# Short last tiles of a mixture of experts by plain float32 matmuls on column groups, and an overflow count taken in mid-kernel

## The chip, the cores and the metric

The kernel runs on one core of a Trainium2 chip. The metric is the device time of one execution in microseconds (us). The engines are named as the profile names them: PE (TensorE, matmuls; PEld its weight loads), DVE (VectorE), ACT (ScalarE), POOL (GpSimd) and SP (SyncE, which here issues the DMAs). PSUM is the memory that matmuls write; it has eight banks of 512 float32 numbers in each of 128 partitions.

## What is computed

Attention within chunks of 64 tokens, and behind it a mixture of experts in which a gate with noise sends each of 4608 tokens to two of eight experts:

```python
def _moe_ref(x, w_gate, w_noise, noise, w1, w2) -> np.ndarray:
    logits = x @ w_gate
    noise_scale = np.log1p(np.exp(x @ w_noise))
    noisy_logits = logits + noise_scale * noise
    top2 = np.argpartition(-noisy_logits, 2, axis=1)[:, :2]
    ...
    for e in range(E):
        for k in range(2):
            mask = top2[:, k] == e
            ...
            h = np.maximum(x[mask] @ w1[e], 0.0)
            out[mask] += top2_w[mask, k, None] * (h @ w2[e])
```

Here x is 4608 x 512, W1 of an expert 512 x 1024 and W2 1024 x 512, all float32.

## The kernel before

The first quarter of the kernel is the attention (`attend`, L593), in token tiles of 128, together with the gate and the scattering of token rows to lists in DRAM, one list for each expert. From about 166 us on the expert layers run. The experts are taken in slots 0 to 7, sorted by how many tokens they have, and each slot has a fixed capacity (`CAPS`, L30): 1216 rows for slots 0 and 1, 1184 for 2 to 4, 1152 for 5 to 7. What does not fit is done by a loop at the end that runs only if the count of overflowing tiles is above zero (L773; it is zero here).

A capacity is cut into tiles of 128 rows, and the tiles into three blocks for each expert (`blocks_of`, L39). 1216 rows leave a last tile of 64 rows, 1184 one of 32, and 1152 none. Such a last tile is the fourth tile of its expert's third block.

Every matrix product is made of three matmuls. A float32 number is split into a high part and a rest, both of type float32r: `hi` is a copy made by ACT, `lo` the difference made by DVE (`w_split`, L113, for weights; L276 and L277 for hidden values). `three` (L256) then multiplies hi by hi, hi by lo and lo by hi. In layer 1 (`layer1`, L265) a piece of W1 is the stationary operand, and the rows of the whole block, 384 to 448, stream past it: 96 matmuls a block. In layer 2 (`layer2`, L286) a tile of hidden values, 128 deep and r rows wide, is stationary, and W2 streams past it in 512 columns, which makes 24 matmuls a tile whatever r is. `weigh` (L280) scales the tile by the gate's weights on DVE, and POOL adds it to the output by an indirect DMA (`store`, L228).

The order of the work is written out by hand; each engine runs its instructions in program order. The main loop (L678) has an iteration for each block i, and in it layer 1 of block i and then layer 2 of block i - 1. Work for later is hung between the matmuls by hooks:

- the next block's x tiles are transposed and split (`x_tile`, L237), in layer 1 or, in the iteration of an expert's second block, in layer 2 of its first one; each such turn lets SP gather one more tile, seven tiles ahead (`gather_more`, L220);
- raw W2 of an expert is split during layer 1 of its second block (L697), and raw W1 of the next expert during layer 2 of its second block, which runs in the iteration of the third (L704).

Raw weights lie in four buffers of the pool `stage` (L97), 512 KB each, used in turn: four pieces of W2 of expert e, then four of W1 of e + 1, then four of W2 of e + 1. `w_load` (L103) issues a load on SP, and it waits there until the buffer's last reader is done. W1 of the next expert is issued at the head of the iteration of the second block (L682), W2 of the next expert at the end of the iteration of the third (L751).

A count read into a register (`values_load`, L772, which the profile calls TENSOR_LOAD) is done by every engine for itself. It stands at the very end, behind nine small DVE steps that compute the count (L759 to L770).

Of the kernel before, what the change touches and what calls it, by code (L numbers as in the profile page):

```python
# [8 lines left out]
FT = mybir.dt.float32  # L9
FR = mybir.dt.float32r  # L10
BF = mybir.dt.bfloat16
I32 = mybir.dt.int32
U32 = mybir.dt.uint32
AF = mybir.ActivationFunctionType
OP = mybir.AluOpType
AX = mybir.AxisListType
# [3 lines left out]
P = 128  # L20
NTOK = 4608
NT = NTOK // P
DM = 512
NE = 8
FF = 1024
ND = DM // P
NF = FF // P
# [8 lines left out]
CLEAN = max(CAPS) - P  # L36


def blocks_of(cap):  # L39

    rows = [min(P, cap - s) for s in range(0, cap, P)]
    out, cur = [], []
    for j, r in enumerate(rows):
        cur.append((j, r))
        if len(cur) == 3 and len(rows) - j - 1 != 1:
            out.append(cur)
            cur = []
    if cur:
        out.append(cur)
    return out  # L50


# [1 line left out]
def kernel(ctx, tc, qT, kT, vh, wgn, noise, w1, w2, out, caps=CAPS):  # L54
    nc = tc.nc
    consts = ctx.enter_context(tc.tile_pool(name="consts", bufs=1))
# [16 lines left out]
    e_row = consts.tile([P, NE], FT, name="e_row")  # L73
# [10 lines left out]
    cape = consts.tile([P, NE], FT, name="cape")  # L84
# [3 lines left out]
    for c in sorted(set(caps[1:])):  # L88
        n = caps.index(c, 1)
        nc.vector.memset(caprow[:, n:n + caps[1:].count(c)], float(c))  # L90
    nc.vector.memset(caprow[:, 0:1], float(caps[0]))
    run8 = consts.tile([P, NE], FT, name="run8")
# [5 lines left out]
    W = {}  # L98
    staged = {}
# [3 lines left out]
    def w_load(e, which, c):  # L103
        st = stage.tile([P, 1024], FT, name="st")
        staged[e, which, c] = st
        if which == 1:
            nc.sync.dma_start(st, w1v[ds(place[e], 1), c].rearrange("o j r f -> (o j) r f") if e else w1[e, c * P:(c + 1) * P, :])  # L107
        else:
            nc.sync.dma_start(st.rearrange("p (f n) -> p f n", f=2),
                              w2[ds(place[e], 1) if e else slice(0, 1), 2 * c * P:(2 * c + 2) * P, :]  # L110
                              .rearrange("o (f p) n -> p (o f) n", f=2))
# [14 lines left out]

    blocks = [blocks_of(c) for c in caps]
    nb = len(blocks[0])  # L130
    assert all(len(b) == nb for b in blocks)
    BL = [(e, b) for e in range(NE) for b in range(nb)]
    NBL = len(BL)
# [6 lines left out]
    NPE = nb  # L140
# [14 lines left out]
    XG, XH, HT, BX, BH, OB = {}, {}, {}, {}, {}, {}  # L155
# [14 lines left out]
    def weights_of(i, j):  # L170
        e = BL[i][0]
        k = j - blocks[0][i][0][0] if i in EARLY else 0
        return lwt0[i][:, k:k + 1] if i in EARLY else lwt[:, j, e:e + 1]
# [37 lines left out]
    def gather(i):  # L211
        for k in range(len(blocks[BL[i][0]][BL[i][1]])):
            gather_tile(i, k)
# [42 lines left out]
    def three(p, w, w_s, x, x_s, first, last, flip=False):  # L256

        (wh, wl), (xh, xl) = w, x
        for n, (a, b) in enumerate(((wh, xh), (wh, xl), (wl, xh)) if not flip else ((wh, xh), (wl, xh), (wh, xl))):
            a, b = a[w_s], b[x_s]  # L260
            if flip:
                a, b = b, a
            nc.tensor.matmul(p, a, b, start=first and n == 0, stop=last and n == 2)  # L263

    def layer1(i, hook, hook_d=lambda f, d: None):  # L265
        e, b = BL[i]
        n = sum(r for _, r in blocks[e][b])
        HT[i] = BH[0 if i == 1 else i % 2]
        for f in range(NF):
            p = bank("l1", (0, 1) if i == 0 else None)[:, 0:n]  # L270
            for d in range(ND):
                three(p, W[e, 1, d], (slice(None), slice(f * P, (f + 1) * P)),
                      XH[i], (slice(None), d, slice(0, n)), d == 0, d == ND - 1)
                hook_d(f, d)
            hh, hl = HT[i][f]
            nc.scalar.activation(hh[:, 0:n], p, AF.Relu)  # L276
            nc.vector.scalar_tensor_tensor(hl[:, 0:n], p, 0.0, hh[:, 0:n].bitcast(FT), op0=OP.max, op1=OP.subtract)  # L277
            hook(f)

    def weigh(i, j, r, p):  # L280
        e = BL[i][0]
        o = OB[0].tile([P, DM], FT, name="o")
        nc.vector.tensor_scalar(o[0:r], p[0:r], weights_of(i, j)[0:r], None, op0=OP.mult)  # L283
        store(i, e, j, r, o)

    def layer2(i, hook):  # L286
        e, b = BL[i]
        tiles = blocks[e][b]
        for k, (j, r) in enumerate(tiles):
            p = bank("l2")  # L290
            for f in range(NF):
                three(p[0:r], W[e, 2, f // 2], (slice(None), slice((f % 2) * DM, (f % 2) * DM + DM)),
                      HT[i][f], (slice(None), slice(k * P, k * P + r)), f == 0, f == NF - 1, flip=True)
                hook(k, f)
            weigh(i, j, r, p)


    pa = ExitStack()
    pk = ExitStack()
# [377 lines left out]

    for i in range(NBL + 1):  # L678
        e, b = BL[i] if i < NBL else (NE, 0)
        if i == 2:  # L680
            gather_more(2)
        if b == 1 % nb and e + 1 < NE and i > 1:  # L682
            for c in range(4):
                w_load(e + 1, 1, c)
        split2 = halves if i < NBL and (b == 1 % nb if e else b == 0) else []
        nxt = blocks[BL[i + 1][0]][BL[i + 1][1]] if i + 1 < NBL else []

        def turn_next(k):
            x_tile(i + 1, k)
            ahead[0] -= 1  # L690
            gather_more(2)

        def hook1(f):
            if i > 1 and b != 1 and f % 2 == 1 and f // 2 < len(nxt):
                turn_next(f // 2)
            if split2:
                w_split(e, 2, *split2[f])  # L697
            if i == 0:
                scatter(2, HT[0][f][0][0:1, 0:1].bitcast(FT))

        def hook2_f(k, f):
            if i > 1 and b == 1 and f % 4 == 1 and 2 * k + f // 4 < len(nxt):
                turn_next(2 * k + f // 4)
            if (k, f) == (0, 3):  # L704
                for q in split1:
                    w_split(split1_e, 1, *q)

        def hook2_r(k, f):
            hook2_f(k, f)
            step_route(2)  # L710
            if f % 2 == 0:
                scatter(1)
            if (k, f) in TURNS[i]:
                x_tile(i + 1, TURNS[i].index((k, f)))

        if 1 < i < NBL and i == 3:
            resolve_all()
            layer2(i - 1, hook2_f)
        if i < NBL:
            layer1(i, hook1, hook_tail if i == 0 else lambda f, d: None)  # L720
        split1 = halves if (i < NBL and b == nb - 1 and e + 1 < NE) else []
        split1_e = e + 1

        if i == 0:
            pa.close()
            block_x(1)
            OB[0] = pb.enter_context(tc.tile_pool(name="ob", bufs=4))
        if i == 0:
            zero_out(NT)
            resolve_early(0)  # L730
            layer2(0, hook2_r)
            finish_route()
            last_rows.close()
            block_h(1)
            for r in range(1, NE):
                place[r] = nc.values_load(order[0:1, r:r + 1], engines=[mybir.EngineType.SP], min_val=0, max_val=NE - 1)
            for c in range(4):
                w_load(1, 1, c)
            pg.close()
            later_xg.append(pb.enter_context(tc.tile_pool(name="xg2", bufs=3)))  # L740
            xy = pb.enter_context(tc.tile_pool(name="xy", bufs=2))
            gather(3)
            for r in range(NE):
                nc.sync.dma_start(meta[:, :, r], by_slot[0:NJ * P, ds(place[r], 1) if r else slice(0, 1), CODE:USED]
                                  .rearrange("(j p) o c -> p j (o c)", p=P))
        elif i == 1:
            resolve_early(1)
            layer2(1, hook2_r)
        elif i != 2 and i != 3:
            layer2(i - 1, hook2_f)  # L750
        if split1:  # L751
            for c in range(4):
                w_load(e + 1, 2, c)
# [1 line left out]


    ovp = ctx.enter_context(tc.tile_pool(name="ovp", bufs=1))
    nf = ovp.tile([P, NE], FT, name="nf")
    nc.vector.tensor_sub(nf, run8, e_row)  # L759
    nc.vector.tensor_scalar(nf, nf, 1.0 / NE, float(P - 1), op0=OP.mult, op1=OP.add)  # L760
    nc.vector.tensor_sub(nf, nf, cape)
    nt = ovp.tile([P, NE], I32, name="nt")
    nc.vector.tensor_copy(nt, nf)
    nc.vector.tensor_scalar(nt, nt, 7, None, op0=OP.arith_shift_right)
    nc.vector.tensor_copy(nf, nt)
    nc.vector.tensor_scalar(nf, nf, 0.0, None, op0=OP.max)
    tot = ovp.tile([1, 1], FT, name="tot")
    nc.vector.tensor_reduce(tot, nf[0:1], AX.X, OP.add)
    toti = ovp.tile([1, 1], I32, name="toti")
    nc.vector.tensor_copy(toti, tot)  # L770
    MT = 80
    n_over = nc.values_load(toti[0:1, 0:1], min_val=0, max_val=MT)  # L772
    with tc.If(n_over > 0):  # L773
        it_row = ovp.tile([P, MT], FT, name="it_row")
        nc.gpsimd.iota(it_row, pattern=[[1, MT]], base=0, channel_multiplier=0, allow_small_or_imprecise_dtypes=True)
# [112 lines left out]
```

## Time and profile before

| | us |
|---|---|
| median of 3 runs | 1030.37 (1027.99 to 1031.94) |
| the profiled execution | 1029.36 |
| its span | 1027.6 |
| PE busy in the span | 983.1 (96%) |
| DVE, ACT, POOL busy | 446.1 (43%), 271.3 (26%), 227.4 (22%) |
| DMA from HBM and to it | 81.69 MB read, 50.13 MB written |

The span runs from the first to the last instruction that the profile saw. Ends of matmuls are modelled and overlap, so the time between the starts of two matmuls tells what one costs, and their "mean ns" does not. A float32 matmul (not float32r) shows as two records.

### The profile page before, as it was taken

The page shows a single profiled execution, that of the slowest core. Times are in us where ns is not written, and L with a number is a line of the kernel's source. Part 1 is how long each engine was busy: PE and PEld are TensorE (multiplying, and loading weights), DVE is VectorE, ACT ScalarE, POOL GpSimd, SP SyncE. Part 2 cuts the span into 40 slices and gives each one's busy share as a digit, 9 for nine tenths or more (in the row PEclk, how much of TensorE's full clock was granted, in tenths as well). Part 3 has the DMA queues.
Part 4 walks back from the last instruction along what each step waited for, and adds up shares of the span by engine and source line. Part 5 has one row for each costly group of instructions (what it writes and reads, how often), then busy time and mean ns, then how long its engine had stood idle before and what let it go on. Part 6 is the DMA issues. An engine that isn't in the chain of part 4 may idle for free.

```text
span 1027.6 us, 16132 instructions
## 1 busy us (share of the span) xinstructions
PE 983.1 (96%) x5962; PEld 883.5 (86%) x5962; DVE 446.1 (43%) x1005; ACT 271.3 (26%) x542; POOL 227.4 (22%) x332
## 2 busy tenths in 40 slices
PE   6889998999799999999999999999999999999996
PEld 6778887898689889888988998899889998999884
DVE  6656665522525443344334432453245324533311
ACT  3434443211314121222222321232123212322100
POOL 3034754751020111111111102101211111101112
PEclk9999999999899999999999999999999999999998
DMA  8899999864561552264225422553244324412213
GB/s 226 259 292 298 328 323 396 310 177 121 88 166 56 124 117 37 60 140 116 40 46 138 124 40 44 125 135 59 36 121 123 74 43 126 120 21 32 31 21 43
DMA packets 103218, 132.93 MB, mean 129 GB/s; under 512 B 22848, under 2 KB 56000, under 8 KB 103136
## 3 DMA queue, kind: packets, MB, share of 16 engines
q1 hardware_dynamic: 86704, 93.54, 30.4%
q0 software_dynamic: 16432, 38.33, 19.1%
q8 instruction: 48, 0.79, 0.3%
q14 instruction: 34, 0.28, 0.1%
HBM read 81.69 MB, written 50.13 MB: 128 GB/s over the span
## 4 chain that ended last, share of the span: by engine, by line
PE 84%; SPq 6%; DMA 5%; DVE 2%; issue 2%; ACT 1%; POOL 0%; DVEq 0%; ACTq 0%; POOLq 0%
PE PS L263 78%; DMA kb<-in_kT 2%; PE PS L381 2%; SPq L322 1%; PE PS L355 1%; SPq L327 1%; DMA xg<-slots 1%; DMA vb<-in_vh 1%; SPq L207 1%; PE PS L409 1%; PE PS L371 1%; SPq L320 1%; DMA out<-zero 1%; PE PS L396 1%; SPq L107 0%
## 5 line engine op out<-in xcount | busy, mean ns | idle before, releaser
L263 PE MATMUL PS<-xh,w1h 128*128 128x384 f32 (+2 forms) x768 | 262.6, 342 | 9.4 <-DVE hl L277 6.2
L230 POOL DMA_INDIRECT out<-o,lid x77 | 119.3, 1549 | 684.5 <-DVE o L283 680.3
L263 PE MATMUL PS<-xh,w1l 128*128 128x384 f32 (+2 forms) x768 | 261.7, 341 | 0.0
L263 PE MATMUL PS<-xl,w1h 128*128 128x384 f32 (+2 forms) x768 | 261.6, 341 | 0.0
L263 PE MATMUL PS<-w2h,hh 128*128 128x512 f32 x616 | 240.5, 390 | 0.0
L263 PE MATMUL PS<-w2h,hl 128*128 128x512 f32 x616 | 240.2, 390 | 0.0
L263 PE MATMUL PS<-w2l,hh 128*128 128x512 f32 x616 | 240.2, 390 | 0.0
L276 ACT ACTIVATE hh<-PS 128x384 fp32r<-128x384 f32 (+2 forms) x192 | 95.0, 496 | 481.0 <-PE PS L263 425.4
L277 DVE SCALAR_TENSOR_TENSOR hl<-PS,hh 128x384 fp32r<-128x384 f32 (+2 forms) x192 | 108.5, 566 | 188.4 <-ACT hh L276 185.5
L283 DVE TENSOR_SCALAR o<-PS,lwt 128x512 f32<-128x512 f32 x77 | 57.7, 749 | 248.6 <-PE PS L263 246.2
L263 PEld LDWEIGHTS PS<-xh,w1h 128*128 128x128 f32 x768 | 145.3, 189 | 12.7 <-DVE hl L277 6.6
L263 PEld LDWEIGHTS PS<-xl,w1h 128*128 128x128 f32 x768 | 145.4, 189 | 1.9
L263 PEld LDWEIGHTS PS<-xh,w1l 128*128 128x128 f32 x768 | 145.2, 189 | 1.1
L263 PEld LDWEIGHTS PS<-w2h,hl 128*128 128x128 f32 x616 | 112.9, 183 | 27.2
L263 PEld LDWEIGHTS PS<-w2l,hh 128*128 128x128 f32 x616 | 112.9, 183 | 26.2
L263 PEld LDWEIGHTS PS<-w2h,hh 128*128 128x128 f32 x616 | 112.9, 183 | 25.8
L532 POOL DMA_INDIRECT slots<-xs,lii x72 | 72.5, 1007 | 26.5 <-issue 20.8
L253 ACT ACTIVATE xh<-y 128x512 fp32r<-128x512 f32 x67 | 41.2, 614 | 105.5 <-DVE y L250 105.5
L254 DVE TENSOR_TENSOR xl<-y,xh 128x512 fp32r<-128x512 f32 x67 | 44.9, 670 | 47.9 <-ACT xh L253 47.2
L355 PE MATMUL PS<-kb,qb 128*64 128x128 f32 x576 | 40.9, 285 | 13.3 <-DMA kb<-in_kT 12.6
L250 DVE STREAM_TRANSPOSE y<-xg 128x512 f32<-128x512 f32 x67 | 45.6, 681 | 11.9 <-DMA xg<-slots 11.9
L381 PE MATMUL PS<-vb,pts 128*64 128x130 f32 x576 | 39.8, 278 | 9.3 <-ACT xt L400 5.6
(114 smaller groups left out, 686.7 us busy)
## 6 DMA issues: line engine op xcount, KB each, us to landing
st<-in_w SPq DMA_DIRECT2D x64, 512.0 KB
xg<-slots SPq DMA_DIRECT2D x252, 64.0 KB
out<-zero SPq DMA_DIRECT2D x37, 256.0 KB
vb<-in_vh SPq DMA_DIRECT2D x72, 130.0 KB
qb<-in_qT SPq DMA_DIRECT2D x36, 256.0 KB
kb<-in_kT SPq DMA_DIRECT2D x72, 128.0 KB
xg<-slots SPq DMA_DIRECT2D x9, 256.0 KB
slots<-zero SPq DMA_DIRECT2D x8, 257.5 KB
```

The costliest lines, as they stand in the source:

```text
L207: nc.sync.dma_start(x[32 * q:32 * q + 32, 0:4 * r].rearrange("p (t c) -> p t c", c=P), by_slot[j * P:j * P + r, ds(place[e], 1), q * P:(q ...
L230: s = nc.gpsimd.indirect_dma_start(out=out, out_offset=bass.IndirectOffsetOnAxis(ap=rows_of(i, j)[0:r], axis=0), in_=o[0:r], in_offset=Non ...
L250: nc.vector.transpose(y[:, 0:4 * r], x[:, 0:4 * r])
L253: nc.scalar.activation(oh, src, AF.Copy)
L254: nc.vector.tensor_sub(ol, src, oh.bitcast(FT))
L263: nc.tensor.matmul(p, a, b, start=first and n == 0, stop=last and n == 2)
L276: nc.scalar.activation(hh[:, 0:n], p, AF.Relu)
L277: nc.vector.scalar_tensor_tensor(hl[:, 0:n], p, 0.0, hh[:, 0:n].bitcast(FT), op0=OP.max, op1=OP.subtract)
L283: nc.vector.tensor_scalar(o[0:r], p[0:r], weights_of(i, j)[0:r], None, op0=OP.mult)
L355: nc.tensor.matmul(PS[s, t % 2, hp * P:(hp + 1) * P], QB[t][:, hp, s], KB[t % RING][:, :, hp, s], start=True, stop=True)
L381: nc.tensor.matmul(PS[s, 3 + hp // 2, o:o + 130], PT[t][:, hp, s], VB[t % RING][:, :, c, hp, :], start=True, stop=True)
L532: s = nc.gpsimd.indirect_dma_start(out=slots, out_offset=bass.IndirectOffsetOnAxis(ap=lii[:, k, t0 + r:t0 + r + 1], axis=0), in_=XS[(t0 + ...
```

## The change

Four things are changed.

`blocks_of` puts an expert's short last tile into its first block and no longer into the third, for slots 1 to 7; slot 0 is as it was.

The layer 2 of such a tile (`apart`: slots from 1 on, fewer than 128 rows) is done by 8 plain float32 matmuls. Layer 1 writes the tile's hidden values once more, unsplit, into a buffer `hr` (an ACT instruction for each of the eight row groups of 128), and the raw W2 in `stage` is the moving operand. The 8 products are summed in 128 / r separate sums, each in a group of r columns of the array and r partitions of PSUM; `weigh` adds the groups up on DVE.

Since raw W2 is now read in layer 2 of the first block, the load of the next expert's W1 is issued behind that layer and no longer at the head of the iteration.

The overflow count is computed at the head of iteration 6 and loaded by all engines at the head of iteration 23, the last block's; the test of it stays at the end.

```diff
-def blocks_of(cap):
+def blocks_of(cap, first):
...
+    rows = [(j, min(P, cap - s)) for j, s in enumerate(range(0, cap, P))]
+    n = -(-(len(rows) - 1) // 3)
+    out = [rows[3 * b:3 * b + 3] for b in range(n)]
+    if len(rows) > 3 * n:
+        out[0 if first else -1].append(rows[-1])
     return out
...
+    def apart(i, r):
+        return i >= NPE and r < P and P % r == 0
...
             nc.scalar.activation(hh[:, 0:n], p, AF.Relu)
+            if apart(i, r):
+                nc.scalar.activation(HR[0][:, f, 0:r], p[:, n - r:n], AF.Relu)
...
-        nc.vector.tensor_scalar(o[0:r], p[0:r], weights_of(i, j)[0:r], None, op0=OP.mult)
+        w = weights_of(i, j)[0:r]
+        nc.vector.tensor_scalar(o[0:r], p[0:r], w, None, op0=OP.mult)
+        for q in range(r, P if apart(i, r) else r, r):
+            nc.vector.scalar_tensor_tensor(o[0:r], p[q:q + r], w, o[0:r], op0=OP.mult, op1=OP.add)
...
+            if apart(i, r):
+                part = NF * r // P
+                for n in range(part):
+                    for q in range(P // r):
+                        f = q * part + n
+                        nc.tensor.matmul(p[q * r:q * r + r], HR[0][:, f, 0:r],
+                                         staged[e, 2, f // 2][:, (f % 2) * DM:(f % 2) * DM + DM], start=n == 0, stop=n == part - 1)
...
+        if i == 6:
+            nf, toti = overflow()
+        if i == NBL - 1:
+            n_over = nc.values_load(toti[0:1, 0:1], min_val=0, max_val=MT)
...
-        if b == 1 % nb and e + 1 < NE and i > 1:
-            for c in range(4):
-                w_load(e + 1, 1, c)
...
         elif i != 2 and i != 3:
             layer2(i - 1, hook2_f)
+        if b == 1 and e + 1 < NE and i > 1:
+            for c in range(4):
+                w_load(e + 1, 1, c)
...
-    n_over = nc.values_load(toti[0:1, 0:1], min_val=0, max_val=MT)
     with tc.If(n_over > 0):
```

PE around the short tile of slot 2, before (the end of the third block; `w2h` and `w2l` are the split W2, `hh` and `hl` the split hidden values; the first six of 24 rows of the short tile):

```order
L263 MATMUL PS<-w2l_4509,hh_2258 128x512
L263 MATMUL PS<-w2h_4508,hl_2259 128x512
L263 MATMUL PS<-w2h_4406,hh_2244 32x512
L263 MATMUL PS<-w2l_4407,hh_2244 32x512
L263 MATMUL PS<-w2h_4406,hl_2245 32x512
L263 MATMUL PS<-w2h_4406,hh_2246 32x512
L263 MATMUL PS<-w2l_4407,hh_2246 32x512
L263 MATMUL PS<-w2h_4406,hl_2247 32x512
```

And now, at the end of the first block (`st` is raw W2, `hr` the unsplit hidden values):

```order
L259 MATMUL PS<-w2l_4528,hh_2258 128x512
L259 MATMUL PS<-w2h_4527,hl_2259 128x512
L303 MATMUL PS<-st,hr 32x512 x8
L259 MATMUL PS<-xh_2239,w1h_4063 128x384
L259 MATMUL PS<-xl_2240,w1h_4063 128x384
```

The 24 matmuls of the tile have become 8, and layer 1 of the expert's third block follows them directly.

SP at the load of W1 for slot 3, in the iteration of slot 2's second block, with the semaphores waited for, before:

```order
L207 DMA xg<-slots 32x4x128 [waits DMAHW3_49]
L107 ISA
L107 DMA st<-in_w 128x1x1024 [waits DMAHW4_49,DVE_49]
L107 ISA
L107 DMA st<-in_w 128x1x1024 [waits DMAHW5_49,DVE_49]
L107 ISA
L107 DMA st<-in_w 128x1x1024 [waits DMAHW6_49,DVE_49]
```

And now:

```order
L203 DMA xg<-slots 32x4x128 [waits DMAHW3_49]
L103 ISA
L103 DMA st<-in_w 128x1x1024 [waits DMAHW4_49,PE_49,Activation_49]
L103 ISA
L103 DMA st<-in_w 128x1x1024 [waits DMAHW5_49,PE_49,Activation_49]
L103 ISA
L103 DMA st<-in_w 128x1x1024 [waits DMAHW6_49,PE_49,Activation_49]
```

The load stands 32 rows later in SP's queue, behind the gathers of layer 2 of the first block, and it waits for PE where it waited for DVE.

PE at the head of the last block's layer 1, where the count is now loaded; before, no row stood between the two L259:

```order
L259 MATMUL PS<-w2l_8252,hh_2816 128x512
L259 MATMUL PS<-w2h_8251,hl_2817 128x512
L718 TENSOR_LOAD toti [waits DVE_49]
L259 MATMUL PS<-xh_2646,w1h_7823 128x384 [waits Activation_49]
L259 MATMUL PS<-xl_2647,w1h_7823 128x384 [waits DVE_49]
```

The load of the count has moved from behind the last matmul to this place; on ACT, DVE, POOL and SP it has moved in the same way.

More of the change, by code (lines that the diff above doesn't have):

```diff
@@ L36 @@
 CLEAN = max(CAPS) - P
-def blocks_of(cap):
[L41 to L49, printed above, removed]
+def blocks_of(cap, first):
[4 more added lines that the diff above has]
+        out[0 if first else -1].append(rows[-1])
     return out
@@ L125 @@
     gate = pg.enter_context(tc.tile_pool(name="gate", bufs=1, side="right"))
-    blocks = [blocks_of(c) for c in caps]
+    blocks = [blocks_of(c, e > 0) for e, c in enumerate(caps)]
     nb = len(blocks[0])
@@ L263, in three @@
             nc.tensor.matmul(p, a, b, start=first and n == 0, stop=last and n == 2)
+    HR = {}
+    def apart(i, r):
+        return i >= NPE and r < P and P % r == 0
     def layer1(i, hook, hook_d=lambda f, d: None):
@@ L267, in layer1 @@
         n = sum(r for _, r in blocks[e][b])
+        r = blocks[e][b][-1][1]
         HT[i] = BH[0 if i == 1 else i % 2]
@@ L290, in layer2, with overflow @@
             p = bank("l2")
[L291 to L294, printed above, removed]
-            weigh(i, j, r, p)
+            if apart(i, r):
[5 more added lines that the diff above has]
+                                         staged[e, 2, f // 2][:, (f % 2) * DM:(f % 2) * DM + DM], start=n == 0, stop=n == part - 1)
+                for f in range(NF):
+                    hook(k, f)
+            else:
+                for f in range(NF):
+                    three(p[0:r], W[e, 2, f // 2], (slice(None), slice((f % 2) * DM, (f % 2) * DM + DM)),
+                          HT[i][f], (slice(None), slice(k * P, k * P + r)), f == 0, f == NF - 1, flip=True)
+                    hook(k, f)
+            weigh(i, j, r, p)
+    MT = 80
+    def overflow():
+        nf = consts.tile([P, NE], FT, name="nf")
+        nc.vector.tensor_sub(nf, run8, e_row)
+        nc.vector.tensor_scalar(nf, nf, 1.0 / NE, float(P - 1), op0=OP.mult, op1=OP.add)
+        nc.vector.tensor_sub(nf, nf, cape)
+        nt = consts.tile([P, NE], I32, name="nt")
+        nc.vector.tensor_copy(nt, nf)
+        nc.vector.tensor_scalar(nt, nt, 7, None, op0=OP.arith_shift_right)
+        nc.vector.tensor_copy(nf, nt)
+        nc.vector.tensor_scalar(nf, nf, 0.0, None, op0=OP.max)
+        tot = consts.tile([1, 1], FT, name="tot")
+        nc.vector.tensor_reduce(tot, nf[0:1], AX.X, OP.add)
+        toti = consts.tile([1, 1], I32, name="toti")
+        nc.vector.tensor_copy(toti, tot)
+        return nf, toti
     pa = ExitStack()
@@ L741 @@
             xy = pb.enter_context(tc.tile_pool(name="xy", bufs=2))
+            HR[0] = pb.enter_context(tc.tile_pool(name="hr", bufs=1)).tile([P, NF, 64], FT, name="hr")
             gather(3)
@@ L757 @@
     ovp = ctx.enter_context(tc.tile_pool(name="ovp", bufs=1))
[L758 to L772, printed above, removed]
     with tc.If(n_over > 0):
```

## The prediction

> **What bounds the kernel now.** I read the page's busy shares first, then the chain that ended last, then the busy times of one stretch, then the places that the change touches.
>
> ```profile
> span 1027.6 us, 16132 instructions
> PE 983.1 (96%) x5962; PEld 883.5 (86%) x5962; DVE 446.1 (43%) x1005; ACT 271.3 (26%) x542; POOL 227.4 (22%) x332
> ...
> 266.19 751.39 PE PS L263 x3744
> 1017.60 0.75 DVE o L283
> ...
> 295.35:1017.57 722.22, 722.22 (x3625) 649.58 (x3623) 287.42 (x467) 172.65 (x336) 106.17 (x134) 1.00 0.37 79
> ```
>
> The last 751 us before the end of the matmuls are one unbroken piece of the chain, all of it matmuls of L263. In the stretch from 295.35 to 1017.57 the five figures are PE, weight loads, DVE, ACT and POOL: PE is busy for all 722.22 us at full granted clock (1.00), DVE for 40% and ACT for 24%, and the DMA engines are 37% occupied. So a microsecond of PE time taken out there comes off the end, and one that PE waits is added. Everything that the change does to ACT, DVE, POOL and SP counts only if PE comes to wait for it.
>
> **The short tiles, as they are.** The last tile of expert slots 1 to 4 has 64, 32, 32 and 32 rows. Its cost is read from the first matmuls of neighbouring groups:
>
> ```profile
> 380.81 0.33 PE L263 MATMUL PS<-xh,w1h 128*128 128x384 f32 x1
> ...
> 397.47 0.39 PE L263 MATMUL PS<-w2h,hh 128*128 128x512 f32 x1
> ...
> 413.83 0.40 PE L263 MATMUL PS<-w2h,hh 128*64 128x512 f32 x1
> ...
> 419.35 0.33 PE L263 MATMUL PS<-xh,w1h 128*128 128x384 f32 x1
> ...
> 519.64 0.39 PE L263 MATMUL PS<-w2h,hh 128*32 128x512 f32 x1
> ...
> 525.21 0.34 PE L263 MATMUL PS<-xh,w1h 128*128 128x384 f32 x1
> ```
>
> The first column is the start. A layer-1 block of 384 rows takes 397.47 - 380.81 = 16.66 us, three full layer-2 tiles 413.83 - 397.47 = 16.36, the 64-row tile 419.35 - 413.83 = 5.52 and a 32-row tile 525.21 - 519.64 = 5.57. A short tile costs as much as a full one (16.36 / 3 = 5.45). The change removes 24 matmuls in each of four tiles: 5.52 + 3 x 5.57 = 22.23 us.
>
> **What stands there instead: 8 plain float32 matmuls of 512 columns on groups of 64 or 32 columns.** Float32 on 64-column groups is in the trace, in the attention stage (L355 and L381, alternating between two groups); these are consecutive pieces of the chain, start and length:
>
> ```profile
> 111.70 1.02 PE PS L355 x16
> 112.72 0.89 PE PS L381 x16
> 113.61 0.59 PE PS L371 x4
> 114.19 0.44 PE PS L396 x4
> ```
>
> L381 issues 8 matmuls of 130 columns for a token tile, and 16 are counted: a float32 matmul is two records. The 8 take 0.89 us. Scaled by columns, 8 matmuls of 512 take 0.89 x 512 / 130 = 3.50 us; any fixed part of the 0.89 would make this less, so it is an upper bound for two groups. Entering and leaving column groups costs extra. The four transposes of L371 right behind L381 take 0.59, the same four of L396 behind them 0.44: 0.15 to leave. L355, which enters, takes 1.02 against 0.89 with fewer columns: 0.13, say 0.15. So 0.30 a tile, and the 64-row tile costs 3.80.
>
> For 32 rows four groups work side by side, which no row of before shows. If they overlap as two do, half the records stand one behind the other: 1.75 + 0.30 = 2.05 us. If four gain nothing over two, it is 3.80 again. On the whole array a 128-column float32 record (L396) takes 0.44 / 4 = 110 ns, against 0.89 / 16 = 56 with two groups: two groups halved it with nothing lost, so I take 2.05 and keep 3.80 for the range. The Trainium skill, "TensorE: Matmul & The Clock Gate", Measured speedup vs the span model, gives three column groups 2.38 times one, not 3; at 79% of ideal, an estimate from that page, the three 32-row tiles would cost 0.46 us more each and the sum would be 1.4 us higher.
>
> PE: -22.23 + 3.80 + 3 x 2.05 = **-12.3 us** (all at 3.80: -7.0). Layer 1 keeps its columns, moved from an expert's third block to its first: 0.
>
> **Work beside it.** ACT gets 32 extra activations (eight in each of four blocks), DVE ten multiply-adds (three for each 32-row tile, one for the 64-row tile). The nearest rows are larger in size:
>
> ```profile
> L276 ACT ACTIVATE hh<-PS 128x416 fp32r<-128x416 f32 x24 | 12.3, 512 | 48.3 <-issue 28.8 <-PE PS L263 19.5
> ...
> L283 DVE TENSOR_SCALAR o<-PS,lwt 32x512 f32<-32x512 f32 x3 | 2.2, 737 | 14.4 <-PE PS L263 14.4
> ```
>
> At most 8 x 0.51 = 4.1 us a block on ACT, beside layer 1 of over 16 us in which ACT is busy for a quarter, and 3 x 0.74 = 2.2 us on DVE behind a short tile. Layer 1 has four PSUM banks in turn, some 2 us each, so a DVE that is 2.2 us late holds nothing up; without that cover it would be 2.2 x 3 + 0.7 = 7 us. Cost 0. The nine small DVE steps of the overflow count (under 2 us) go to the same idle time.
>
> **The moved weight load.** A slot of `stage` with raw W2 is now read until the short tile ends, so the four W1 pieces of the next expert are issued at that moment (call it T0) and no longer in layer 1 of the second block. From T0 PE has a layer-1 block and three layer-2 tiles to do, 16.66 + 16.36 = 33.0 us, and then needs the new W1. Before, the four were issued over 13 us as slots came free; only at expert slot 1 were they issued at once:
>
> ```profile
> 425.56 13.03 SPq L107 DMA_DIRECT2D st<-in_w  x4
> ...
> 233.65 5.48 SPq L107 DMA_DIRECT2D st<-in_w  x4
> 239.93 24.67 SPq L207 DMA_DIRECT2D xg<-slots  x12
> ...
> 251.29 12.09 DMA xg<-slots
> ...
> 235.10:261.70 26.60, 24.91 (x123) 21.48 (x121) 4.47 (x7) 2.68 (x5) 4.31 (x6) 1.00 0.49 124
> ...
> 470.97 4.26 ACT L120 ACTIVATE w1h<-st 128x512 fp32r<-128x512 f32 x8
> ...
> 471.63 4.91 DVE L121 TENSOR_TENSOR w1l<-st,w1h 128x512 fp32r<-128x512 f32 x8
> ```
>
> There the gather queued right behind the four landed at 251.29 + 12.09 = 263.38, 29.7 us after the first was issued, and I take that as the latest for the four. The last piece then needs two halves split: an ACT half (4.26 / 8 = 0.53) and two DVE halves (1.23), 1.8 us. Ready at T0 + 31.5, needed at T0 + 33.0: hidden, with 1.5 us to spare in the worst case that the trace shows. Queued behind the waiting load on SP are gathers of tiles seven turns ahead, and then W2, needed another block later; behind the split on DVE is the weighing of three tiles, each with a PSUM bank of its own. Cost 0, with the rival below. Slots 5 and 6 have no short tile and load earlier.
>
> **The overflow count.** Now at the end:
>
> ```profile
> 1018.63 1.56 POOL L230 DMA_INDIRECT out<-o,lid  x1 [3.84 <-DVE nf L760]
> ...
> L772 POOLq TENSOR_LOAD <-toti x1: 567/567/567, 1020.3 to 1020.3; - x1
> L772 PEldq TENSOR_LOAD <-toti x1: 612/612/612, 1020.4 to 1020.4; - x1
> ...
> L773 POOLq COMPARE_BRANCH  x1: 53/53/53, 1021.0 to 1021.0; - x1
> ...
> L884 POOLq DRAIN  x3: 46/107/4235, 1022.5 to 1027.3; - x3
> ```
>
> POOL's last store ends at 1020.2, its branch comes at 1021.0, and a drain of 4.2 us ends the run. Without the load of the count, the branch and all behind it come up to 0.8 us earlier; if the drain waits for the store's data, 0. I take -0.5. In the middle PE must load the count in 0.61 us at most; if the matmuls queued ahead cover it, 0. I take +0.3.
>
> **Sum.** -12.3 - 0.5 + 0.3 = -12.5. The profiled execution took 1029.36 us (span 1027.6 and 1.8 around it), so it would become 1016.9; the median of the runs, 1030.37, lies 1.0 higher: **1017.9 us**.
>
> **Rivals.** (1) *Four groups are no faster than two.* A matmul's two records use the same columns. If starts keep program order, the next group's first record starts beside this one's second, and the rate is one matmul for each record's time however many groups there are. Two groups look the same either way (0.89), so the trace cannot tell. Every short tile costs 3.80: -7.0 - 0.2 = -7.2, 1023.2 us. The Trainium skill, "TensorE: Matmul & The Clock Gate", The mechanism, says that matmuls start and end strictly in program order; by that rule this rival holds, and no run here shows it yet.
>
> (2) *The W1 load becomes the wait.* All four pieces start 33.0 us before their use, where the only burst shown took 29.7 with gathers and stores beside it. PE waits if they land later than T0 + 31.2; each microsecond is paid four times (slots 1 to 4). It gives the 12.5 back at T0 + 34.3 and is slower by over 0.5% (5.2 us) from T0 + 35.6; at T0 + 37 it is 4 x 5.8 = 23 us of waits and 1041 us. For it: gathers, stores and W2 share the DMA engines, and the margin is 1.5 us. Against it: the DMA engines were 49% occupied during that burst (235.10 to 261.70, last but one figure of its row) and 37% over the later stretch with its loads included.
>
> (3) *The gain does not reach the end*, because DVE or ACT becomes the bound: 1030. Against it are 40% and 24% busy.
>
> **How the numbers follow.** A measurement of this kernel can tell about 0.5%, 5.2 us. Forecast 0.70 (faster); rival 1 0.17 (faster, by 0.7%, perhaps 0.01 within 0.5%); rival 2 0.11, of which 0.03 still faster, 0.03 within 0.5%, 0.05 slower; rival 3 0.02 (same, or slower by the added waits). Faster 0.88, same 0.06, slower 0.06. Range: below, no cost for changing groups (4 x 0.3), the tail's 0.8 and PE's load at 0 make -14.3, and the runs of before scatter by 2 us: 1014.5. Above, rival 1 and a microsecond of scatter: 1024.5.
>
> **What would show it.** The new matmuls: about 1.75 us from first to last start for 32 rows, 3.5 for 64; near 3.5 for both means rival 1. The chain should stay one piece of PE from about 266 us on. A layer-1 block of slots 2 to 5 that starts after idle time released by DVE w1l or ACT w1h is rival 2. The new PE load of the count should leave under 0.6 us between its neighbours, and POOL's branch should follow its store at once. I am wrong if the 32-row tiles cost over 3.8, or if PE waits anywhere behind 295 us.

## The result, and the profile after

The changed kernel takes 1016.58 us (median of 6 runs, 1013.9 to 1020.57), the kernel before in the same series 1029.47 (6 runs, 1027.99 to 1031.94). The ratio is 0.9872, 95% interval 0.9847 to 0.9898: faster, by more than the 0.5% that can be told. The profiled execution took 1013.9 us.

The page after, its span, busy times and chain, and then the stretch that answers to the window of before, from the first layer 1 of slot 1 to the last matmul:

```profile
span 1011.6 us, 16090 instructions
PE 971.4 (96%) x5930; PEld 874.3 (86%) x5930; DVE 453.9 (45%) x1015; ACT 275.8 (27%) x574; POOL 227.5 (22%) x332
...
1004.33 1.56 POOL out L226
```

```profile
293.29:1003.26 709.97, 709.97 (x3593) 640.52 (x3591) 296.31 (x484) 176.11 (x367) 106.25 (x134) 1.00 0.36 81
```

PE is busy for all 709.97 us of the stretch at full clock, as it was for 722.22 before: 12.25 us are gone, and no wait has taken their place. The chain has lost its long piece of matmuls. It now stops at POOL's last store at 1004.33, because POOL's test of the count no longer hangs on the end of the work (the chain of tail_only, below, stops at its last store too), so the window has to carry the reading instead. The span is shorter by 16.0 in three parts:

- ahead of the stretch 295.35 - 293.29 = 2.1 us, which is scatter: blocks_only (below), whose work up to that point is that of the changed kernel, has it at 298.26, and tail_only, whose work there is that of the kernel before, at 294.34;
- the stretch 12.25;
- behind the last matmul 10.0 (1027.6 - 1017.57) before and 8.3 (1011.6 - 1003.26) now: 1.7.

Without the scatter that is 13.9; the medians differ by 12.9.

The short tiles and their neighbours (start, length; x16 are the two records of eight matmuls), and the last block, at whose head the count is loaded:

```profile
329.41 0.39 PE L259 MATMUL PS<-w2h,hh 128*128 128x512 f32 x1
345.86 3.65 PE L303 MATMUL PS<-st,hr 128*64 128x512 f32 x16
349.45 0.44 PE L259 MATMUL PS<-xh,w1h 128*128 128x384 f32 x1
366.20 0.39 PE L259 MATMUL PS<-w2h,hh 128*128 128x512 f32 x1
...
449.92 1.93 PE L303 MATMUL PS<-st,hr 128*32 128x512 f32 x16
451.77 0.45 PE L259 MATMUL PS<-xh,w1h 128*128 128x384 f32 x1
...
953.52 0.39 PE L259 MATMUL PS<-w2h,hl 128*128 128x512 f32 x1
953.75 0.33 PE L259 MATMUL PS<-xh,w1h 128*128 128x384 f32 x1
...
970.42 0.39 PE L259 MATMUL PS<-w2h,hh 128*128 128x512 f32 x1
```

From start to next start the 64-row tile takes 349.45 - 345.86 = 3.59 us and the 32-row tile 451.77 - 449.92 = 1.85. The three tiles ahead take 345.86 - 329.41 = 16.45 instead of 16.36, and the layer 1 behind 366.20 - 349.45 = 16.75 instead of 16.66: 0.09 on each side of the tile. One_group (below), which uses a single column group, has the same 0.09 on both sides, so it goes with the switch to these matmuls and not with the number of groups. The last block's layer 1 takes 970.42 - 953.75 = 16.67, and its first matmul follows its neighbour in 0.23: the load of the count costs PE nothing. It was done ahead of time (length in ns, first and last start in us):

```profile
L718 PEldq TENSOR_LOAD <-toti x1: 483/483/483, 949.7 to 949.7; - x1
```

### The profile page after: what moved, and what is told of

Read it like the earlier page. It is cut to its first block, busy times and chain, and to the rows that moved or that the text cites. A ratio compares the mean times of both kernels' runs of the same rounds, so it can differ in the third digit from the quotient of the medians.

```text
span 1011.6 us, 16090 instructions
## 1 busy us (share of the span) xinstructions
PE 971.4 (96%) x5930; PEld 874.3 (86%) x5930; DVE 453.9 (45%) x1015; ACT 275.8 (27%) x574; POOL 227.5 (22%) x332
## 5 line engine op out<-in xcount | busy, mean ns | idle before, releaser
L259 PE MATMUL PS<-xh,w1h 128*128 128x384 f32 (+2 forms) x768 | 262.8, 342 | 9.0 <-DVE hl L281 7.3
L259 PE MATMUL PS<-xl,w1h 128*128 128x384 f32 (+2 forms) x768 | 261.7, 341 | 0.0
L259 PE MATMUL PS<-xh,w1l 128*128 128x384 f32 (+2 forms) x768 | 261.6, 341 | 0.0
L259 PE MATMUL PS<-w2h,hh 128*128 128x512 f32 x584 | 227.9, 390 | 0.0
L259 PE MATMUL PS<-w2h,hl 128*128 128x512 f32 x584 | 227.7, 390 | 0.0
L259 PE MATMUL PS<-w2l,hh 128*128 128x512 f32 x584 | 227.6, 390 | 0.0
L259 PEld LDWEIGHTS PS<-xh,w1h 128*128 128x128 f32 x768 | 145.4, 189 | 15.1 <-DVE hl L281 7.7
L259 PEld LDWEIGHTS PS<-xl,w1h 128*128 128x128 f32 x768 | 145.3, 189 | 1.7
L259 PEld LDWEIGHTS PS<-xh,w1l 128*128 128x128 f32 x768 | 145.3, 189 | 1.1
L259 PEld LDWEIGHTS PS<-w2h,hl 128*128 128x128 f32 x584 | 109.2, 187 | 23.5
L259 PEld LDWEIGHTS PS<-w2l,hh 128*128 128x128 f32 x584 | 109.2, 187 | 22.5
L259 PEld LDWEIGHTS PS<-w2h,hh 128*128 128x128 f32 x584 | 109.2, 187 | 22.5
L246 DVE STREAM_TRANSPOSE y<-xg 128x512 f32<-128x512 f32 x67 | 45.6, 681 | 13.1 <-DMA xg<-slots 13.1
L416 PE MATMUL PS<-vb,pts 128*64 128x130 f32 x576 | 40.4, 279 | 10.5 <-ACT xt L435 3.6
```

Source lines behind the costliest of these rows:

```text
L246: nc.vector.transpose(y[:, 0:4 * r], x[:, 0:4 * r])
L416: nc.tensor.matmul(PS[s, 3 + hp // 2, o:o + 130], PT[t][:, hp, s], VB[t % RING][:, :, c, hp, :], start=True, stop=True)
```

## The experiments

**The theories.** *Theory:* the gain is the number of column groups that run side by side, each group a queue of its own, and 1.7 us come from the moved count; the other edits cost and bring nothing. *Rival 1:* matmuls start in program order, so the second record of one matmul holds the next group up. *Rival 2:* the moved W1 load is at its limit. *A last rival:* some of the gain comes from the tile's new place in the first block.

Ratios are against the kernel before on the same chip. The tile times come from the traces, start of the tile to start of the next layer 1; differences of the rounded starts shown below can be 0.01 off.

| run | time, us | ratio (95%) | 64-row tile | 32-row tile |
|---|---|---|---|---|
| the changed kernel | 1016.58 | 0.9872 (0.9847 to 0.9898) | 3.58 | 1.85 |
| tail_only | 1028.03 | 0.9980 (0.9966 to 0.9994) | 5.52 | 5.56 |
| blocks_only | 1028.52 | 0.9991 (0.9974 to 1.0008) | 5.52 | 5.56 |
| two_groups | 1019.79 | 0.9908 (0.9883 to 0.9933) | 3.58 | 3.56 |
| one_group | 1033.27 | 1.0050 (1.0027 to 1.0073) | 7.01 | 6.98 |
| group_major | 1018.70 | 0.9874 (0.9848 to 0.9899) | 5.35 | 1.87 |
| runs_of_two | 1015.71, one run | | 3.64 | 1.87 |
| runs_of_three | 1019.15, one run | | 4.49 | 1.87 |
| w1_later | 1023.99 | 0.9932 (0.9908 to 0.9957) | 3.58 | 1.85 |
| gather_first | 1009.12 | 0.9778 (0.9756 to 0.9799) | 3.58 | 1.85 |

**tail_only: the kernel before with the overflow count moved, and nothing else.**

```diff
+        if i == 6:
+            nf, toti = overflow()
+        if i == NBL - 1:
+            n_over = nc.values_load(toti[0:1, 0:1], min_val=0, max_val=MT)
...
-    n_over = nc.values_load(toti[0:1, 0:1], min_val=0, max_val=MT)
```

> The kernel before with one part of the change alone: the overflow count computed at the head of iteration 6 and loaded by all engines at the head of iteration 23. Theory (the gain is PE time of the short tiles, 12.2 us, and the end, 1.7 us by the two traces): the time between the last matmul's end and the end of the span falls from 10.0 us to about 8.4, PE shows no gap at the head of the last block, and the run is 1.5 to 2 us below the kernel before. Rival (the end got shorter by chance): 10.0 us again, and no difference.

The ratio says 2.1 us less (0.6 to 3.5), which holds the 1.7 of the profile. What stands behind the last matmul, first of before, then of the changed kernel (min, median and longest in ns, first and last start in us):

```profile
L773 POOLq INC_SWDGE_SEM  x1: 1186/1186/1186, 1021.3 to 1021.3; - x1
```

```profile
L798 POOLq COMPARE_BRANCH  x1: 53/53/53, 1004.1 to 1004.1; - x1
...
L798 POOLq INC_SWDGE_SEM  x1: 1176/1176/1176, 1004.4 to 1004.4; - x1
...
L909 POOLq DRAIN  x3: 46/112/5200, 1005.6 to 1011.3; - x3
```

And of tail_only, its span, its last matmul, its last store and the same three steps:

```profile
span 1024.8 us, 16122 instructions
...
1016.17 0.39 PE L263 MATMUL PS<-w2h,hl 128*128 128x512 f32 x1
```

```profile
1017.62 1.56 POOL L230 DMA_INDIRECT out<-o,lid  x1 [3.84 <-POOLq L780]
```

```profile
L780 POOLq COMPARE_BRANCH  x1: 53/53/53, 1017.4 to 1017.4; - x1
L780 POOLq INC_SWDGE_SEM  x1: 1186/1186/1186, 1017.7 to 1017.7; - x1
...
L891 POOLq DRAIN  x3: 46/113/4986, 1018.9 to 1024.4; - x3
```

Before, POOL ended its store at 1020.2, loaded the count, branched at 1021.0, spent 1.19 us on INC_SWDGE_SEM and then drained for 4.2. With the count loaded early POOL branches ahead of its last store (1017.4 against 1017.62 in tail_only, 1004.1 against 1004.33 in the changed kernel), and INC_SWDGE_SEM runs beside the store. The drain then starts when the store is about to end and takes 5.0 to 5.2 us. In tail_only 1024.8 - 1016.6 (the end of its last matmul, 1016.17 + 0.39) leaves 8.2 us, near the 8.3 of the changed kernel, against 10.0: the moved count brings 1.7 to 1.8.

**blocks_only: the changed kernel, but the short tiles by 24 split matmuls as before.** They lie in the first block, W1 is loaded late, and the count is moved.

```diff
-        return i >= NPE and r < P and P % r == 0
+        return False
```

> The changed kernel, with the short tiles kept in the first block and W1 loaded behind layer 2, but computed by the 24 split matmuls as before. Theory: moving a tile to another block is worth nothing, so each short tile takes 5.5 us again and only the end's 1.7 us remain: 1028 us against 1029.5 before. Rival (a part of the gain comes from the new order of blocks and loads): more than 3 us below the kernel before.

```profile
456.55 0.39 PE L259 MATMUL PS<-w2h,hh 128*32 128x512 f32 x1
...
462.11 0.34 PE L259 MATMUL PS<-xh,w1h 128*128 128x384 f32 x1
```

```profile
298.26:1020.49 722.23, 722.23 (x3625) 649.61 (x3623) 288.57 (x474) 172.35 (x335) 106.17 (x134) 1.00 0.36 80
```

The 32-row tile costs 462.11 - 456.55 = 5.56 us there too. The stretch from the first layer 1 of slot 1 to the last matmul (second fence) takes 722.23 us, and before the change it took 722.22; the time is that of tail_only within the intervals. The new place of the tile and of the W1 load is worth nothing by itself, and the last rival falls.

**two_groups and one_group: the sums of a 32-row tile on two groups of columns instead of four, and of every short tile on one.** The number of matmuls stays at 8; fewer multiply-adds are left on DVE.

```diff
+    def groups_of(r):
+        return min(2, P // r)      # one_group: return 1
...
-                part = NF * r // P
+                part = NF // groups_of(r)
-                    for q in range(P // r):
+                    for q in range(groups_of(r)):
```

> The changed kernel, where the 32-row tiles use two column groups in place of four (four float32 matmuls for each group, the rest alike). Theory (column groups run side by side, as many as there are): a 32-row tile takes 8 records of 427 ns one behind the other and about 0.15 us, 3.6 us in place of 1.85; three tiles, so 5.2 us above the changed kernel and about 7 below the kernel before. Rival (the rate is set by something else than the groups, such as reading W2): 1.85 us again.

> The changed kernel with all 8 float32 matmuls of a short tile in a single column group, one sum. Theory: 16 records of 427 ns one behind the other, 7.0 us a tile, which is 5.1 above the changed kernel's for each 32-row tile and 3.4 for the 64-row tile, 18.7 us in all; that puts it at about 1035, 6 us slower than the kernel before. Rival (float32 itself is cheap, and the groups add little): at or below 5.5 us a tile, so not slower than before.

The 32-row tile of slot 2 and the layer 1 behind it, in two_groups, then in one_group:

```profile
450.86 3.63 PE L306 MATMUL PS<-st,hr 128*32 128x512 f32 x16
454.42 0.44 PE L259 MATMUL PS<-xh,w1h 128*128 128x384 f32 x1
```

```profile
454.52 7.05 PE L306 MATMUL PS<-st,hr 128*32 128x512 f32 x16
461.51 0.44 PE L259 MATMUL PS<-xh,w1h 128*128 128x384 f32 x1
```

One group takes 6.98 us, two 3.56, four 1.85, as the theory had it: two groups are 1.96 times as fast as one and four 3.77 times. On one group the eight plain float32 matmuls cost more than the 24 they replace (6.98 against 5.56), and the kernel is slower than before, by 0.5%. The whole gain on PE is the groups'. Rival 1 falls with this: by it four groups would take as long as two. In the changed kernel's 32-row tile four records start between 449.92 and 449.94, where rival 1 has one alone for the first 0.43 us (view of 449.90 to 449.94):

```profile
449.92 0.64 PE L303 MATMUL PS<-st,hr 128*32 128x512 f32 x4
```

The tiles alone make two_groups 3 x 1.71 = 5.1 us slower than the changed kernel and one_group 3.4 + 3 x 5.13 = 18.8; by the ratios it is 3.7 (with 2.6 us of uncertainty on each ratio) and 18.3.

**group_major, runs_of_two, runs_of_three: the same matmuls in another order.** In the changed kernel each matmul goes to another group than the one ahead of it. Here the matmuls of one group stand together: all of them, two at a time, three at a time.

```diff
-                for n in range(part):
-                    for q in range(P // r):
+                for q in range(P // r):
+                    for n in range(part):
```

> The changed kernel with the two inner loops exchanged: all matmuls of one column group are issued before the next group's first. In the 32-row tile a group's four records follow each other, 427 ns each. Theory A (a waiting matmul holds up all behind it, except that one may wait for each group): a group is nearly done when the next begins, so the tile takes between 3 records and 13 records of 427 ns, and I put it at about 10, 4.3 us; the 64-row tile, 8 records in each of two groups, at about 15, 6.4 us; in all 3 x 2.4 + 2.9 = 10 us above the changed kernel. Theory B (each group has a queue of its own, deep enough for four records): 1.85 and 3.6 us as in the changed kernel.

The 64-row tile (two groups, four matmuls each), then a 32-row tile (four groups, two each):

```profile
350.70 5.42 PE L303 MATMUL PS<-st,hr 128*64 128x512 f32 x16
356.06 0.45 PE L259 MATMUL PS<-xh,w1h 128*128 128x384 f32 x1
...
456.55 1.94 PE L303 MATMUL PS<-st,hr 128*32 128x512 f32 x16
458.42 0.45 PE L259 MATMUL PS<-xh,w1h 128*128 128x384 f32 x1
```

The 32-row tiles lose next to nothing (1.87): the last group's first record starts 0.04 us after the first group's, though six matmuls stand ahead of it. The 64-row tile loses 1.77. The trace does not name the group of a record, but the starts fall into two rows of eight, each 0.43 us apart. In the first row they are 350.70, 351.18, 351.61, 352.04 and 352.47, and only then, at 352.48, the second row begins. So theory B holds for the 32-row tiles alone, and theory A's 10 us are far off. What fits both tiles is that a group takes in four records, the running one with them, and that what comes behind a full group waits. (Four records are two of these matmuls; the runs do not tell one count from the other.) If that is so, two matmuls at a time cost nothing and three cost two records, 2 x 0.43 us:

> The matmuls of one group of columns are issued two at a time (group 0 twice, group 1 twice, and so on). Theory, from the run with each group's matmuls one behind the other, where the second group of the 64-row tile began when the fifth of the first group's eight records began: each group can hold four records, the running one with them, and issue goes on to the next group until one is full. Two matmuls are four records, so nothing stops: 64-row tile 3.58 us from its first start to the next layer-1 start, 32-row tiles 1.87, as when issued in turn. Rival: a group that is not the first waits whenever more than one matmul of the same group stands ahead of it, so that the 64-row tile costs one matmul's two records (0.86 us) more or more than that: 4.4 and over.

> The same, three matmuls of one group at a time (the 64-row tile: group 0 three times, group 1 three times, then one each; the 32-row tiles have two matmuls a group and so go group by group). Theory of four records held by a group: the second group begins when the third of the first group's six records begins, two record spacings late (2 x 0.43 us), and ends as much later: 64-row tile 3.58 + 0.86 = 4.44 us; 32-row tiles 1.87. Rival (order within the tile matters only when a group's whole sum is issued at once, 5.35): 3.58.

```profile
347.80 3.71 PE L304 MATMUL PS<-st,hr 128*64 128x512 f32 x16
351.44 0.44 PE L259 MATMUL PS<-xh,w1h 128*128 128x384 f32 x1
```

```profile
350.23 4.56 PE L304 MATMUL PS<-st,hr 128*64 128x512 f32 x16
354.72 0.44 PE L259 MATMUL PS<-xh,w1h 128*128 128x384 f32 x1
```

3.64 (first fence, two at a time) and 4.49 (three), where 3.58 and 4.44 were expected; the 32-row tiles take 1.87 in both. The depth of four records, found in group_major, fits all four orders. The Trainium skill, "TensorE: Matmul & The Clock Gate", The mechanism, has matmuls start and end strictly in program order; by the starts above they do not here, since in group_major the second group's first record starts (352.48) ahead of the first group's last three (352.90 to 353.76), which stand before it in the program.

**w1_later: the four W1 loads moved later still, into layer 1 of the third block.**

```diff
+            if b == 2 and 0 < e < NE - 1 and f == 3:
+                for c in range(4):
+                    w_load(e + 1, 1, c)
...
-        if b == 1 and e + 1 < NE and i > 1:
-            for c in range(4):
-                w_load(e + 1, 1, c)
```

> The changed kernel with the next expert's W1 loaded later: in layer 1 of the third block, behind its fourth group of rows, 8.3 us after the end of the short tile, for slots 1 to 6 alike. Theory (in the changed kernel the last piece is split 29.1 us after the short tile's end and needed 34.8 us after it, so 5.7 us are to spare): PE waits 2.6 us at the head of layer 1 of slots 2 to 7, 16 us in all, released by DVE w1l, and the kernel is at about 1032. Rival (the load has more room than that, as it goes faster when issued later): no wait and 1016.6. If the margin were gone already in the changed kernel, PE would wait 8 us each time, 50 us in all.

First the load for slot 3 in the changed kernel, the splits of its last piece on ACT and on DVE, and the layer 1 that needs them:

```profile
451.95 6.54 SPq L103 DMA_DIRECT2D st<-in_w  x4
```

```profile
479.49 1.16 ACT L116 ACTIVATE w1h<-st 128x512 fp32r<-128x512 f32 x2 [4.14 <-DMA st<-in_w]
...
480.16 1.29 DVE L117 TENSOR_TENSOR w1l<-st,w1h 128x512 fp32r<-128x512 f32 x2 [4.00 <-ACT w1h L116]
```

```profile
484.89 0.35 PE L259 MATMUL PS<-xh,w1h 128*128 128x416 f32 x1
```

Then w1_later, its load for slot 5, the head of that slot's layer 1, all waits of PE and ACT for `w1h`, and 3.3 us behind PE's wait at slot 5 (last but two figure: granted clock):

```profile
670.95 5.28 SPq L103 DMA_DIRECT2D st<-in_w  x4
```

```profile
695.36 0.33 PE L259 MATMUL PS<-xh,w1h 128*128 128x384 f32 x1
...
699.50 0.45 PE L259 MATMUL PS<-xh,w1h 128*128 128x384 f32 x1 [2.39 <-ACT w1h L116]
...
716.64 0.39 PE L259 MATMUL PS<-w2h,hh 128*128 128x512 f32 x1
```

```profile
ACT w1h L116 <- DMA st<-in_w: 80.5, 18, 6.0
PE PS L259 <- ACT w1h L116: 5.4, 4, 2.4
```

```profile
701.20:704.50 3.30, 3.30 (x12) 3.30 (x12) 2.02 (x4) 0.47 (x2) 2.40 (x3) 0.50 0.84 221
```

Issued 8 us later, the load is waited for. In the profiled run the first layer 1 of slots 2 to 7 is longer by 0.2, 0.9, 0, 4.6, 3.9 and 1.8 us (for slot 5: 716.64 - 695.36 = 21.28 instead of 16.67). That is 11.4 in sum, in a run that was the slowest of five (1029.37); by the ratios the median lost 6 us. Only 5.4 of the 11.4 are PE's waits. Behind two of them, 2.4 us at slot 5 and 1.7 at slot 6, PE's granted clock was 0.50 for 3.4 us, which costs another 1.7 us each time; behind the 1.2 us at slot 7 it stayed at 1.00. The rest is not broken down. The theory had 15.6, and it had slots 2 to 4 pay as much as the others, which they did not; why stays open. So the mechanism of rival 2 exists, and the load in the changed kernel stands some 8 us ahead of where slots 2 to 4 begin to pay.

**gather_first: the one wait that is left.** Both kernels lose time in one place, the layer 1 of slot 0's last block (28.2 us before, 29.3 now). Here the gather and the small loads that stood behind four W1 loads on SP are put ahead of them.

```diff
-            for c in range(4):
-                w_load(1, 1, c)
             pg.close()
...
             gather(3)
...
+            for c in range(4):
+                w_load(1, 1, c)
```

> The changed kernel with one more edit, in the only place behind 200 us where both traces show PE waiting: at the end of slot 0's first iteration the gathers for slot 1's first block and the loads of their meta data are issued ahead of the four W1 loads and no longer behind them. Theory (the first gather lands at 263 us because it queues behind 2 MB of W1 that 4 of 16 DMA engines move): it lands some 15 us earlier, PE's 6 to 8 us of waiting there and the slow clock behind it go, layer 1 of that block takes 19.5 us in place of 28, and the kernel falls by up to 8.8 us, to about 1008. Rival (the gather waits for the scatters, not for W1): no change. A danger: W1, now 10 us later, must be split by 286 us, and lands at about 275.

In the changed kernel that block, from its start to the end of PE's wait, and behind it (last but two figure: granted clock), and its waits:

```profile
242.10:264.00 21.90, 14.72 (x73) 13.30 (x71) 3.86 (x7) 2.59 (x5) 1.60 (x2) 0.88 0.40 114
264.10:271.40 7.30, 7.27 (x24) 6.58 (x25) 4.79 (x8) 2.67 (x5) 0.00 (x0) 0.66 0.65 27
```

```profile
DVE y L246 <- DMA xg<-slots: 13.1, 1, 13.1
...
PE PS L259 <- DVE hl L281: 7.3, 1, 7.3
```

And the same block in gather_first:

```profile
248.70:268.10 19.40, 19.40 (x97) 17.99 (x96) 8.79 (x14) 5.55 (x10) 1.60 (x2) 1.00 0.53 75
```

DVE waited 13.1 us for a gather; the order on DVE made the split of hidden values late, PE waited 7.3 us for that, and after it PE's granted clock was 0.66 for another 7.3. With the gather ahead of the weights both are gone: 19.4 us at full clock instead of 29.3. The ratio is 0.9778 (0.9756 to 0.9799) against 0.9872, 9.7 us less: this kernel beats both. (The Trainium skill, "TensorE: Matmul & The Clock Gate", Part 1: The HAM clock gate, says that PE's clock falls after some 3.4 us of idleness; the trace agrees with a wait of 7.3 us and the 0.66 behind it. In w1_later waits of 2.4 and 1.7 us were enough, so the measurement decides here.)

## Why the prediction was right, step by step

The forecast was 1017.9 us and faster; 1016.6 was measured, inside the range, by the mechanism that the forecast named.

- *What bounds the kernel.* Right. The window shows PE busy without a gap before and after, and 12.25 of the 16.0 us in the span are PE's.
- *24 matmuls a tile, 22.23 removed.* Right: the neighbours of the tile kept their times but for the 0.09 on each side.
- *The 64-row tile, 3.50 + 0.30 = 3.80.* 3.59 + 0.18 = 3.77. Both parts were right. The last pair of records starts at 348.92, 3.06 behind the first; with its own 0.43 the eight matmuls take 3.49, under the bound of 3.50. The other 0.09 of the tile and the 0.18 of its neighbours are the changing over, 0.27 against 0.30. (The attention's products, from which the price was scaled, are plain float32 too; the three matmuls of the kernel's description are those of the expert layers.)
- *The 32-row tiles, 1.75 + 0.30 = 2.05, taken against 3.80.* 1.85 + 0.18 = 2.03. This was the one real choice in the sum. It was argued from two groups that halved a record's time, which did not decide it, as rival 1 said, so that part of the hit was luck; two_groups and one_group decide it.
- *Three groups 2.38 times one (the Trainium skill, "TensorE: Matmul & The Clock Gate", Measured speedup vs the span model).* By it the tiles would have cost 0.46 us more each. Four groups gave 3.77 times one group, and 1.85 is 0.10 above the ideal 1.75. No run here uses three groups.
- *PE, -12.3.* -12.25 from the windows.
- *Work beside it, 0.* Right. The steps that were bounded by larger rows, in the changed kernel:

```profile
L280 ACT ACTIVATE hr<-PS x32: 188/191/218, 296.4 to 605.7; 128x32 f32<-128x32 f32 x24, 128x64 f32<-128x64 f32 x8
```

```profile
L290 DVE SCALAR_TENSOR_TENSOR o<-PS,lwt,o x10: 741/745/753, 350.4 to 659.0; 32x512 f32<-32x512 f32 x9, 64x512 f32<-64x512 f32 x1
```

```profile
DVE hl L281 <- ACT hr L280: 30.4, 20, 2.4
```

  An extra activation takes 0.19 us, not 0.51, a multiply-add 0.745 as forecast. The last row shows a new releaser that the forecast did not name: DVE's `hl` now waits for ACT's `hr`. PE has no gap in the stretch, so it costs nothing; PE reads `hl` only a layer later.
- *The W1 load, 0 with 1.5 us to spare.* 0 is right, the margin was too small. The split of the last piece starts at 479.49, 27.7 us after the tile's end at 451.77, not 29.7, and its two halves are done on ACT by 480.65 and on DVE by 481.45. The layer 1 that needs them starts at 484.89 and comes to the fourth piece 1.7 us later. The spare is some 3 to 5 us, and w1_later shows that being 8 us later costs.
- *PE's load of the count, +0.3.* The step was mis-sized: 0. PE's sequencer did it at 949.7, 4 us ahead of the matmul behind it (953.75), while queued matmuls ran.
- *The tail, -0.5.* The step was mis-sized: -1.7. The forecast moved the branch up by 0.8 us, to the end of the store. In fact the branch stands ahead of the store, and INC_SWDGE_SEM behind it, 1.18 us that the forecast had no term for, runs beside the store too. The drain gave back 5.2 - 4.2 = 1.0 of that. What the drain waits for was not tried.
- *The sum, -12.5.* The two measured terms make -12.25 - 1.7 = -13.95. By the ratio's interval the kernel is 10.5 to 15.8 us faster, by the medians 12.9; the forecast and the terms both lie in that, and what is left between them is scatter like the 2.1 us ahead of the stretch. The two mis-sized steps moved the sum by 1.5 us in one direction; that the forecast lies only 1.3 us from the median is in part luck, since the six runs lie 6.7 us apart. Two figures beside the sum were added up loosely: the range's terms give 1014.1 and 1024.2, the chances of "faster" 0.89.
- *The signs.* PE does not wait behind 295 us, and the load of the count leaves 0.23 us between its neighbours, as forecast. Two signs came out otherwise without touching the sum: the chain is no longer one piece of PE, and POOL's branch stands ahead of its last store and not behind it.

## What to carry to other kernels

Where PE is the bound and a tile has few rows, the cost to look at is columns streamed, which the number of rows did not change here: 64 and 32 rows cost 5.52 and 5.56 us by split matmuls, 7.01 and 6.98 by float32 ones on one group. The short tile got cheaper when its sum was cut into groups of columns that stream side by side, and of the ways tried here only then. Count the records that a group can hold when ordering the matmuls: take turns between groups, or at most two float32 matmuls of a group in a row. And before changing arithmetic, look for the one place where PE waits: the order of loads on SP was worth 9.7 us here, beside 12.9 for the whole change. A wait can cost more than its length, as the granted clock fell behind the longer ones.

## What the runs showed of the hardware

- Column groups of PE run side by side, and the four orders tried fit a queue of four records for each, the running one included: the 64-row tile took 3.58, 3.64, 4.49 and 5.35 us with one, two, three and four matmuls of a group in a row.
- Going over to float32 matmuls on 64 or 32 columns and back cost the neighbours 0.09 us on each side, with one group as with four.
- A float32 matmul of 512 columns costs 0.87 us on one group (6.98 / 8), more than three float32r ones on the whole array (5.56 / 8 = 0.70).
- At the program's end POOL's branch and its INC_SWDGE_SEM (1.18 us) ran ahead of and beside the last indirect store once nothing held them back; with the count loaded after the store the end was 1.7 us longer.
- PE's granted clock was 0.50 for 3.4 us behind waits of 2.4 and of 1.7 us, and stayed at 1.00 behind one of 1.2 us (w1_later).
